# Weights in pairs of 1024 columns and a second buffer for their sums, in an attention and gated-product kernel

## Chip, core and metric

The kernel runs on one core of a Trainium2 chip. The metric is the device time of one execution in microseconds, the median of several runs. Its engines are PE (matrix products), DVE, ACT and POOL (element-wise work), and SP, whose queue issues all loads and stores.

## What is computed

Attention for 8 batches of 8 heads (576 tokens, head size 64), once over a local window and once over tokens averaged in fours, and then a gated product of the joined heads x (4608 x 512). Cut to what matters:

```python
def _attn_ref(q, k, v):
    q_d = q.reshape(B, H, Sd, factor, D).mean(axis=3)
    ...
    out_d = sm_attn(q_d, k_d, v_d)
    out_up = np.repeat(out_d, factor, axis=2)
    mask = np.abs(pos[:, None] - pos[None, :]) < factor
    scores = scale * np.matmul(q, k.transpose(0, 1, 3, 2))
    scores = np.where(mask, scores, -1000000.0)
    ...
    out_local = np.matmul(attn, v)
    return (out_up + out_local).astype(np.float32)

def _moe_ref(x, w_gate, w_val, w_out):
    gate = 1.0 / (1.0 + np.exp(-(x @ w_gate)))
    val = x @ w_val
    return (gate * val @ w_out).astype(np.float32)
```

Weights are 512 x 1536 (gate, value) and 1536 x 512 (out). They reach the kernel as 64-bit floating-point words.

## The kernel before

**Work.** A batch has four units u = 4b + hp, each a pair of heads, whose attention yields one 128-row piece of x (`xs`, split into two f16 parts). The products of a batch run over 12 pieces fc of 128 columns: `pg` (gate) and `pv` (value), 24 matmuls of 128x288 each (both halves of the tokens, 3 matmuls for each of 4 contraction pieces), then `tanh`, the product of both (L723) and its f16 split `gq` (L186 on ACT for the high part, L187 on DVE for the low one); at last the output products `po`, 72 matmuls for each of m = 0 to 3 and both halves. Batches 0 and 1 multiply plainly. Batches 2 to 7 use fewer products over block sums of the weights, which `wring` reads from a DRAM tile `wd` through a ring of three buffers.

**Weights.** There are 36 pieces (k, i), twelve each for gate, value and out. `wload` reads 512 KB (128 x 1024 32-bit words) into one of NST = 4 stage buffers. `wjoin` makes 512 f32 numbers of it: ACT's Prelu on the high word (L237), DVE's shift (L239), DVE's shift and or with the low word (L240); the largest magnitude is taken by ACT (`Abs`, L243) or by DVE (`absmax`, L182). A pair of gate and value pieces, four in all, shares a scale: `wscale` reduces the bounds to two numbers (L253), finds a power of two over all partitions through PE (`mxt`, `mxr`, `mxg`), and sets the gates' scale; `oscale` does it for the output weights. `wsplit` writes the f16 parts, high on ACT (L186), low on DVE (L187). Loads go out in the order of the joins, each new one after a join has freed a buffer.

**Sums.** In batches 0 to 2 `sums(p, k)` runs 12 times: POOL adds both parts of a pair of pieces into x (L779, 128 x 1024), DVE makes four sums of blocks in y (L788), ACT casts y to f16 back into x's place (L791), DVE subtracts for the low part (L792), and SP writes 512 KB to `wd`. There is one x and one y.

**Order.** Every step has a due time in a table T (a position, not a measured time); steps are written out sorted by it, and a scheduler with a model of the engines settles the order on each queue. `j0` to `j35` place the joins, `JBEHIND` with B1, B2, B3 and BO holds a join's shift back behind x3 or a gate product. In listings of an order `pv_1_8_0` is the value product of batch 1, fc 8, first half, and every tile has a number behind its name. Each engine works through its queue in order. The loads of q and k (`load_qk`) use NQK = 3 buffers, and a load waits for the steps `s1` and `prep2` of the unit three before.

The lines on the sum's buffers and on the order of the loads:

```python
        x = place(a, 1024)
        y = place(a + 1024, 1024)
...
    for n, prev in zip(order[NST:], order):
        add(JPOS[prev] + 0.05, lambda n=n: wload(*WORDER[n]))
```

Of the kernel before, what the change touches and what calls it, by code (L numbers as in the profile page):

```python
# [1100 lines left out]
```

## Time and profile before

| | us |
|---|---|
| median of 3 runs | 1007.38 |
| lowest, highest | 1003.67, 1007.9 |
| profiled execution | 1004.63 |
| its span | 1002.9 |
| PE busy | 972.1 (97%) |
| DVE busy | 748.3 (75%) |
| ACT busy | 576.8 (58%) |
| POOL busy | 231.6 (23%) |

The span is the time from the first to the last instruction of the profiled execution; 1.7 us of that execution lie outside it. Busy shares are means over stages of different kinds, so the stages are read one by one: the attention of batch 0 ahead of the first gate product (to 56 us), gates and values of batch 0 (to 140), its outputs (to 198), gates of batch 1 (to 281), its outputs (to 336), and six batches of 110 to 114 us. In the trace, `arena` is the room that holds the weights, x, stage and sum buffers together, `wo` the output weights, `gq` the split gated product, `x` and `od` the two attention results. A matmul record's length contains the time in which it overlaps the next one.

### The profile page before, as it was taken

The numbers are of one execution on the slowest core, as the hardware profiler recorded it, in microseconds if no ns is written. First come the engines' busy times: TensorE is split into PE (matmuls) and PEld (weight loads), VectorE is DVE, ScalarE is ACT, GpSimd is POOL, SyncE is SP. The second block draws the span as 40 slices with busy tenths as digits, with TensorE's granted clock in tenths as the row PEclk, the third lists the DMA queues.
The fourth block names the chain that finished last, engine by engine and source line by source line (L and its number), as shares of the span: only waits on it lengthen the run. The fifth ranks groups of instructions, "written<-read, shape, count | busy, mean of one in ns | idle before, by whom it ended". The sixth has DMA issues, their size and how long they took to land.

```text
span 1002.9 us, 24111 instructions
## 1 busy us (share of the span) xinstructions
PE 972.1 (97%) x9715; PEld 774.5 (77%) x9715; DVE 748.3 (75%) x1495; ACT 576.8 (58%) x1588; POOL 231.6 (23%) x244
## 2 busy tenths in 40 slices
PE   8998999999989899999999999999999999999998
PEld 6786768877767678877788778787788778887776
DVE  6998988568764899848896598948896598737750
ACT  4887677564842687437853486627963487322320
POOL 7300342414225321231203321231203210110000
PEclk9999999999989999999999999999999999999999
DMA  8668930515146355464556455463556444414501
GB/s 341 192 193 276 310 114 31 164 56 158 61 134 202 117 199 174 155 177 156 177 165 178 129 200 174 153 178 127 190 180 164 143 164 156 129 52 157 184 3 46
DMA packets 84224, 156.92 MB, mean 156 GB/s; under 512 B 43536, under 2 KB 49808, under 8 KB 84112
## 3 DMA queue, kind: packets, MB, share of 16 engines
q1 hardware_dynamic: 84112, 155.38, 48.7%
q8 instruction: 76, 1.25, 0.5%
q14 instruction: 36, 0.29, 0.1%
HBM read 127.04 MB, written 20.45 MB: 147 GB/s over the span
## 4 chain that ended last, share of the span: by engine, by line
PE 67%; DVE 12%; DMA 8%; ACT 7%; issue 3%; POOL 2%; SPq 0%; ACTq 0%; DVEq 0%; POOLq 0%
PE po L424 23%; PE pv L424 18%; PE pg L424 18%; DMA v<-in_v_dram 2%; DMA arena<-in_wg_dram 2%; PE s L460 2%; PE x L424 2%; ACT t L496 1%; PE sd L474 1%; PE od L424 1%; DVE vblk L187 1%; DVE arena L788 1%; DVE arena L832 1%; DMA wd<-arena 1%; DMA arena<-in_wv_dram 1%
## 5 line engine op out<-in xcount | busy, mean ns | idle before, releaser
L424 PEld LDWEIGHTS <-arena 128*128 128x128 f16 x4176 | 401.8, 98 | 111.8 <-issue 10.3
L424 PE MATMUL po<-gq,wo 128*128 128x288 f16 x2304 | 294.5, 289 | 5.7 <-ACT gq L186 4.6
L424 PE MATMUL pg<-arena 128*128 128x288 f16 x2088 | 274.5, 286 | 3.8 <-ACT arena L186 1.6
L424 PEld LDWEIGHTS <-wo 128*128 128x128 f16 x2304 | 225.4, 99 | 66.2 <-issue 6.0
L424 PE MATMUL pv<-arena 128*128 128x288 f16 x2088 | 275.0, 286 | 1.5 <-ACT tanh L720 0.5
L832 DVE TENSOR_TENSOR arena<-pv,arena 128x288 f32<-128x288 f32 x252 | 105.8, 450 | 23.5 <-PE pv L424 16.9
L496 ACT ACTIVATE t<-t,mx 128x64 f32<-128x64 f32 x290 | 72.5, 334 | 33.5 <-DVE mx L494 33.4
L832 DVE TENSOR_TENSOR arena<-pg,arena 128x288 f32<-128x288 f32 x180 | 76.8, 449 | 6.6 <-PE pg L424 1.7
L750 DVE TENSOR_SCALAR arena<-po,osc 128x288 f32<-128x288 f32 x32 | 16.5, 514 | 86.2 <-PE po L424 63.4
L752 ACT ACTIVATE arena<-po,osc 128x288 f32<-128x288 f32 x32 | 15.9, 500 | 86.9 <-PE po L424 80.1
L510 ACT ACTIVATE t<-t,sm 128x64 f32<-128x64 f32 x240 | 60.0, 335 | 6.8 <-DVE sm L507 5.5
L449 POOL TENSOR_TENSOR qkh<-qk 128x576 f32<-128x576 f32 x31 | 40.5, 1306 | 93.0 <-DMA qk<-in_qkd_dram 92.1
L187 DVE SCALAR_TENSOR_TENSOR vblk<-v,svb,vblk 64x640 f16<-64x640 f32 x52 | 53.2, 1023 | 6.6 <-ACT vblk L186 5.8
L407 POOL TENSOR_TENSOR vdblk<-vd 64x192 f32<-64x192 f32 x58 | 35.8, 617 | 88.0 <-PE od L424 84.9
L450 POOL TENSOR_TENSOR qks<-qkh 128x288 f32<-128x288 f32 x32 | 26.9, 840 | 113.8 <-PE sd L474 113.4
L632 ACT CAST arena<-arena 128x576 f16<-128x576 f32 (+1 forms) x24 | 21.9, 911 | 54.1 <-DVE arena L626 27.6
L186 ACT ACTIVATE vblk<-v,svb 64x640 f16<-64x640 f32 x52 | 42.8, 823 | 14.2 <-PE x L424 11.0
L535 ACT ACTIVATE e<-sd,mxd 72x144 f32<-72x144 f32 x128 | 46.8, 371 | 0.9
L405 POOL TENSOR_TENSOR vd<-vd 128x384 f32<-128x384 f32 x29 | 26.1, 901 | 88.9 <-DMA vd<-in_vd_dram 88.9
L633 DVE TENSOR_TENSOR arena<-arena 128x576 f16<-128x576 f32 (+1 forms) x24 | 28.3, 1180 | 23.4 <-ACT arena L632 23.3
L653 POOL TENSOR_TENSOR arena<-arena 128x288 f32<-128x288 f32 x12 | 9.6, 796 | 147.1 <-DVE arena L626 147.1
L779 POOL TENSOR_TENSOR arena<-arena 128x1024 f32<-128x1024 f16 x12 | 26.1, 2171 | 59.5 <-DMA wd<-arena 51.1
(140 smaller groups left out, 1331.6 us busy)
## 6 DMA issues: line engine op xcount, KB each, us to landing
arena<-wd SPq DMA_DIRECT2D x72, 896.0 KB, 4.7
qk<-in_qkd_dram SPq DMA_DIRECT2D x31, 576.0 KB, 6.2
vd<-in_vd_dram SPq DMA_DIRECT2D x29, 384.0 KB, 3.9
v<-in_v_dram SPq DMA_DIRECT2D x32, 320.0 KB, 4.5
arena<-in_wg_dram SPq DMA_DIRECT2D x12, 512.0 KB, 4.5
arena<-in_wv_dram SPq DMA_DIRECT2D x12, 512.0 KB, 5.0
arena<-in_wo_dram SPq DMA_DIRECT2D x12, 512.0 KB, 4.9
wd<-arena SPq DMA_DIRECT2D x12, 512.0 KB, 3.1
```

Source lines behind the costliest of these rows:

```text
L186: nc.scalar.activation(hi, src, AF.Copy, scale=sc)
L187: return nc.vector.scalar_tensor_tensor(out=lo, in0=src, scalar=sc, in1=hi, op0=ALU.mult, op1=ALU.subtract)
L405: nc.gpsimd.tensor_tensor(out=x[:, :, 0:2], in0=x[:, :, 0:2], in1=x[:, :, 2:4], op=ALU.add)
L407: nc.gpsimd.tensor_tensor(out=o, in0=x[ps, g, 0], in1=x[ps, g, 1], op=ALU.add)
L424: nc.tensor.matmul(o, w[a], x[c], start=first and i == 0, stop=last and i == len(pairs) - 1)
L449: nc.gpsimd.tensor_tensor(out=y, in0=x[:, :, :, 0:2], in1=x[:, :, :, 2:4], op=ALU.add)
L450: nc.gpsimd.tensor_tensor(out=s["qks"].rearrange("p (a g) -> p a g", a=2), in0=y[:, :, :, 0], in1=y[:, :, :, 1], op=ALU.add)
L496: nc.scalar.activation(t[:, g], t[:, g], AF.Exp, bias=mx[:, g : g + 1], scale=-1.0)
L510: nc.scalar.activation(t[:, g], t[:, g], AF.Copy, scale=sm[:, g : g + 1])
L535: nc.scalar.activation(s["e"][:, qb, h, :], pt[:QM, qb * SD : (qb + 1) * SD], AF.Exp, bias=mx[:, qb : qb + 1], scale=QKSCALE / 16, accum_o ...
L633: eng.tensor_tensor(out=dst_[:, :, 1], in0=src, in1=dst_[:, :, 0], op=ALU.subtract)
L832: eng.tensor_tensor(out=dst_, in0=x, in1=y, op=ALU.add)
```

## The change

- The 36 pieces become 18 pairs. `wload` reads 1 MB into two of the four stage buffers, so two loads can be under way; two are issued ahead, and each further one after a join. Join, bound and split work on 1024 columns.
- The bound of a pair is one number for gate and one for value, so the step `m2` (L253) is gone. `gate_scale` is taken out of `wscale` and placed no earlier than the maxima over v.
- The output splits run in the order 0 to 5, and the output products of batch 0 take fc in the order 0 to 11 instead of `MIXED` (0, 6, 1, 7, ...). The free gap in the output weights' room is no longer used.
- `sums` takes one of two buffers x in turn; y stays single.
- NQK falls from 3 to 2: a load of q and k waits for the unit two before. In batch 0, units 2 and 3 borrow room of the output weights.
- Unused branches of `wsplit` are deleted.
- T is set anew. Among it: T1 (start of batch 1) 193.7 to 196.29, TP 126.05 to 130.14, S0 2.49 to 3.39, SS 9.17 to 9.91, `wl` 1.41 to 9.82, B1 6 to 14, B2 14 to 3, B3 7 to 31, BO 18 to 9. With B1 = 14 no shift of a gate or value join is held back.

```diff
-NQK = 3
+NQK = 2
...
-ARENA = 2 * (NPC + 1) * WPC + 2 * NPAIR * S + NST * 2 * WPC
+ARENA = 2 * (NPC + 2) * WPC + 2 * NPAIR * S + 2 * S + 3 * 1024
...
-        turn[0] += 1
-        return place(AST + (turn[0] - 1) % NST * 2 * WPC, n)
...
+        a = turn[0] % NST
+        turn[0] += 1 if n <= 2 * WPC else 2
+        assert a + (turn[0] - a) % NST <= NST
+        return place(AST + a * 2 * WPC, n)
+
+    def wload(k, p):
+        t = wraw[k, p] = stage(4 * WPC).bitcast(I32).rearrange("p (a b) -> p a b", b=2)
+        load(t.rearrange("p (i a) b -> p i (a b)", i=2), srcs[k][2 * p : 2 * p + 2].bitcast(I32).rearrange("i p c -> p i c"))
...
-        m2 = wk.tile([P, 2 * (b - a)], F32, tag="m2", name=f"m2_{a}", bufs=2)
-        nc.vector.tensor_reduce(m2, hmx[:, 4 * a : 4 * b].rearrange("p (n f) -> p n f", f=2), axis=AX.X, op=ALU.max)
-        pow2(e, m2)
+        pow2(e, hmx[:, 2 * a : 2 * b])
         over(c, e)
-        gate_scale(0, a, b)
...
+    def wsplit(k, p):
...
+        a = wwide(k, p).rearrange("p (f c) -> p f c", f=2)
+        sc = co[:, 2 * p : 2 * p + 1] if k == "o" else cw[:, p, "gv".index(k) : "gv".index(k) + 1]
+        split(home[k][:, 2 * p : 2 * p + 2, 0], home[k][:, 2 * p : 2 * p + 2, 1], a, sc)
...
-            out_group(b, m, h, pts[h], MIXED if b == 0 else range(NFC))
+            out_group(b, m, h, pts[h], range(NFC))
...
-        x = place(a, 1024)
-        y = place(a + 1024, 1024)
+        x = place(a + (len(wready) % 2) * 1024, 1024)
+        y = place(a + 2048, 1024)
...
-        add(max(at(u - 3, "s1") + 0.1, at(u - 3, "prep2") + 0.1, p0 - T["lk"]), lambda u=u: load_qk(u))
+        add(max(at(u - NQK, "s1") + 0.1, at(u - NQK, "prep2") + 0.1, p0 - T["lk"]), lambda u=u: load_qk(u))
...
-    for n, prev in zip(order[NST:], order):
+    for n, prev in zip(order[2:], order):
         add(JPOS[prev] + 0.05, lambda n=n: wload(*WORDER[n]))
...
+        add(p0, lambda a=a, e=e: wscale(a, e))
+        add(max(p0, PV) + 0.01, lambda a=a, e=e: gate_scale(0, a, e))
...
-        add(p + 0.1 + T["os"] * i, lambda n=n: wsplit("o", n))
+    for i in range(NP):
+        add(p + 0.1 + 2 * T["os"] * i, lambda i=i: wsplit("o", i))
```

DVE's queue at the split of the last unit's x, before (`arena<-arena,cw` is a weight split, `xs<-x` the last unit's x, `arena<-xs,sxb` its split; L239 and L240 are shift and or):

```order
L187 SCALAR_TENSOR_TENSOR arena_109<-arena_109,cw_129 128x512
L161 TENSOR_SCALAR mxg4_1074<-ident_103,mxr4_1072 2x2
L187 SCALAR_TENSOR_TENSOR arena_109<-arena_109,cw_129 128x512
L626 TENSOR_TENSOR xs_113<-x_3_8_888,od16_3_880 128x112
L626 TENSOR_TENSOR xs_113<-x_3_0_887,od16_3_880 128x464
L187 SCALAR_TENSOR_TENSOR arena_109<-arena_109,cw_129 128x512 x2
L187 SCALAR_TENSOR_TENSOR arena_109<-xs_113,sxb_135,arena_109 128x576
L239 TENSOR_SCALAR arena_109<-arena_109 128x512 x4
L240 SCALAR_TENSOR_TENSOR arena_109<-arena_109 128x512 x4
```

And now (L237 and L238 are shift and or):

```order
L175 TENSOR_SCALAR cw_129<-ew_128 128x2
L287 TENSOR_SCALAR tsc_136<-ew_128,pvb_133 128x1
L608 TENSOR_TENSOR xs_113<-x_3_8_881,od16_3_878 128x112
L608 TENSOR_TENSOR xs_113<-x_3_0_880,od16_3_878 128x464
L187 SCALAR_TENSOR_TENSOR arena_109<-arena_109,cw_129 128x2x512 x2
L187 SCALAR_TENSOR_TENSOR arena_109<-xs_113,sxb_135,arena_109 128x576
L237 TENSOR_SCALAR arena_109<-arena_109 128x1024
L187 SCALAR_TENSOR_TENSOR arena_109<-arena_109,cw_129 128x2x512
L238 SCALAR_TENSOR_TENSOR arena_109<-arena_109 128x1024
```

In this stretch the four splits of 512 columns have become two of 1024 (two more stand earlier in the queue), and behind x's split four joins of 512 have become one of 1024 between two further splits.

DVE's queue at the values of fc 8 and 9 of batch 1, before (L788 and L792 are a sum's merges, `gq` the split of a gated product, L723 the product with `pv`):

```order
L626 TENSOR_TENSOR arena_109<-x_9_8_3967,od16_9_3856 128x112
L788 TENSOR_TENSOR arena_109<-arena_109 128x256 x2
L187 SCALAR_TENSOR_TENSOR gq_111<-tanh_112,gq_111 128x576
L788 TENSOR_TENSOR arena_109<-arena_109 128x256
L187 SCALAR_TENSOR_TENSOR vblk_123<-v10_2599,svb_134,vblk_123 64x10x64 x2
L788 TENSOR_TENSOR arena_109<-arena_109 128x256
L633 TENSOR_TENSOR arena_109<-arena_109 128x2x288
L723 SCALAR_TENSOR_TENSOR tanh_112<-tanh_112,pv_1_9_0_4046 128x288
L561 TENSOR_TENSOR hl_11_4215<-t_11_3722,hl_11_4215 128x640
L633 TENSOR_TENSOR arena_109<-arena_109 128x4x288
L723 SCALAR_TENSOR_TENSOR tanh_112<-tanh_112,pv_1_9_1_4059 128x288
```

And now (L769 and L773 are the sum's merges, L705 the product with `pv`):

```order
L705 SCALAR_TENSOR_TENSOR tanh_112<-tanh_112,pv_1_8_1_3821 128x288
L543 TENSOR_TENSOR hl_11_4068<-t_11_3568,hl_11_4068 128x640
L769 TENSOR_TENSOR arena_109<-arena_109 128x256 x2
L615 TENSOR_TENSOR arena_109<-arena_109 128x4x288
L182 TENSOR_REDUCE vm3_4357<-v14_4078 128x1
L769 TENSOR_TENSOR arena_109<-arena_109 128x256
L187 SCALAR_TENSOR_TENSOR gq_111<-tanh_112,gq_111 128x576
L705 SCALAR_TENSOR_TENSOR tanh_112<-tanh_112,pv_1_9_0_3897 128x288
L773 TENSOR_TENSOR arena_109<-arena_109 128x4x256
L705 SCALAR_TENSOR_TENSOR tanh_112<-tanh_112,pv_1_9_1_3910 128x288
L769 TENSOR_TENSOR arena_109<-arena_109 128x256 x3
```

One merge stands ahead of the `gq` split of fc 8 where two did, the value splits of unit 10 (`vblk`) have moved further ahead, and a sum's last step and the next sum's merges stand between and behind the products of fc 9.

DVE's queue ahead of the maximum over v of batch 2 (`mxr`, `mxg`) in the output products of batch 1, before:

```order
L788 TENSOR_TENSOR arena_109<-arena_109 128x256 x4
L505 TENSOR_REDUCE sm_12_4622<-t_12_4354 128x10
L792 TENSOR_TENSOR arena_109<-arena_109 128x4x256
L507 RECIPROCAL sm_12_4622<-sm_12_4622 128x10
L750 TENSOR_SCALAR arena_109<-po_1_2_1_4418,osc_137 128x288
L626 TENSOR_TENSOR arena_109<-x_11_0_4466,od16_11_4330 128x464
L626 TENSOR_TENSOR arena_109<-x_11_8_4492,od16_11_4330 128x112
L159 TENSOR_REDUCE mxr11_4515<-mxt11_4513 1x1
L532 TENSOR_REDUCE mxd_12_0_4533<-sd_12_0_4525 72x2
L532 TENSOR_REDUCE mxd_12_1_4617<-sd_12_1_4526 72x2
L161 TENSOR_SCALAR mxg11_4517<-ident_103,mxr11_4515 1x1
```

And now:

```order
L487 TENSOR_REDUCE sm_12_4476<-t_12_4190 128x10
L489 RECIPROCAL sm_12_4476<-sm_12_4476 128x10
L543 TENSOR_TENSOR hl_12_4513<-t_12_4190,hl_12_4513 128x640
L732 TENSOR_SCALAR arena_109<-po_1_2_1_4244,osc_137 128x288
L608 TENSOR_TENSOR arena_109<-x_11_0_4306,od16_11_4205 128x464
L608 TENSOR_TENSOR arena_109<-x_11_8_4332,od16_11_4205 128x112
L514 TENSOR_REDUCE mxd_12_0_4367<-sd_12_0_4359 72x2
L514 TENSOR_REDUCE mxd_12_1_4375<-sd_12_1_4360 72x2
L159 TENSOR_REDUCE mxr11_4385<-mxt11_4383 1x1
L615 TENSOR_TENSOR arena_109<-arena_109 128x2x288
L161 TENSOR_SCALAR mxg11_4387<-ident_103,mxr11_4385 1x1
```

The sum (L788 and L792) that stood in front is gone from here, and a step of x (L615) stands between `mxr` and `mxg`.

## Rows read from the trace of the kernel before

**Rows 1.** Windows: length, busy us of PE PEld DVE ACT POOL, PEclk, DMA share, GB/s.

```profile
56.00:140.00 84.00, 78.21 (x689) 60.38 (x687) 74.97 (x167) 63.40 (x158) 18.51 (x16) 1.00 0.75 245
140.00:198.00 58.00, 56.55 (x651) 45.54 (x650) 43.80 (x102) 35.90 (x104) 20.18 (x24) 0.97 0.30 97
198.00:281.00 83.00, 81.10 (x814) 64.63 (x812) 59.98 (x108) 57.90 (x170) 27.83 (x22) 1.00 0.34 99
281.00:336.00 55.00, 45.44 (x415) 34.51 (x414) 36.25 (x61) 21.76 (x55) 23.27 (x20) 0.91 0.49 156
336.00:450.00 114.00, 113.49 (x1156) 90.90 (x1154) 89.31 (x178) 68.53 (x197) 25.03 (x28) 1.00 0.53 171
```

**Rows 2.** Timeline of PE: start us, us, operation, count, [idle before and releaser].

```profile
55.99 2.37 PE L424 MATMUL pg<-arena 128*128 128x288 f16 x18
...
197.76 3.11 PE L424 MATMUL pg<-arena 128*128 128x288 f16 x24
200.71 2.49 PE L424 MATMUL pv<-arena 128*128 128x288 f16 x19
...
290.09 7.86 PE L424 MATMUL po<-gq,wo 128*128 128x288 f16 x39 [4.62 <-ACT gq L186]
...
329.24 0.38 PE L162 MATMUL mxt<-mxg,ones 1*128 1x1 f32 x2 [2.95 <-DVE mxg L161]
...
336.00 2.25 PE L424 MATMUL pg<-arena 128*128 128x288 f16 x17
```

**Rows 3.** Timeline of DVE around the split of x3.

```profile
56.27 1.40 DVE L187 SCALAR_TENSOR_TENSOR arena<-arena,cw 128x512 f16<-128x512 f32 x2
57.59 0.81 DVE L187 SCALAR_TENSOR_TENSOR arena<-xs,sxb,arena 128x576 f16<-128x576 f32 x1
58.32 1.43 DVE L239 TENSOR_SCALAR arena<-arena 128x512 int32<-128x512 int32 x4
```

**Rows 4.** Timeline of DVE, the merges of sums (L788, L792).

```profile
230.86 2.71 DVE L788 TENSOR_TENSOR arena<-arena 128x256 f32<-128x256 f32 x3 [0.99 <-POOL arena L779]
...
280.22 1.93 DVE L788 TENSOR_TENSOR arena<-arena 128x256 f32<-128x256 f32 x2 [4.28 <-POOL arena L779]
...
283.34 0.41 DVE L788 TENSOR_TENSOR arena<-arena 128x256 f32<-128x256 f32 x1
...
289.24 1.22 DVE L792 TENSOR_TENSOR arena<-arena 128x1024 f16<-128x1024 f32 x1
...
322.48 2.06 DVE L788 TENSOR_TENSOR arena<-arena 128x256 f32<-128x256 f32 x4 [5.74 <-POOL arena L779]
```

**Rows 5.** Timeline of POOL, two adds of sums.

```profile
278.06 2.12 POOL L779 TENSOR_TENSOR arena<-arena 128x1024 f32<-128x1024 f16 x1 [7.68 <-DMA wd<-arena]
...
293.26 2.12 POOL L779 TENSOR_TENSOR arena<-arena 128x1024 f32<-128x1024 f16 x1 [10.46 <-DMA wd<-arena]
```

**Rows 6.** Waits of POOL and of DVE, 190 to 346: us in total, times, longest.

```profile
POOL arena L779 <- DMA wd<-arena: 51.1, 9, 10.5
...
DVE arena L788 <- POOL arena L779: 18.7, 8, 5.7
```

**Rows 7.** Groups by form, DVE to 140 and ACT to 200: count, busy, mean ns, idle before.

```profile
L240 DVE SCALAR_TENSOR_TENSOR arena<-arena 128x512 int32<-128x512 int32 x24 | 17.0, 722 | 0.0
L239 DVE TENSOR_SCALAR arena<-arena 128x512 int32<-128x512 int32 x24 | 10.6, 451 | 3.5 <-ACT arena L237 3.5
...
L182 DVE TENSOR_REDUCE hmx<-arena 128x1 f32<-128x512 f32 x6 | 4.0, 675 | 0.0
...
L237 ACT ACTIVATE arena<-arena 128x512 f32<-128x512 f32 x36 | 24.3, 676 | 24.3 <-DMA arena<-in_wg_dram 9.9 <-DMA arena<-in_wo_dram 8.3 <-DMA arena<-in_wv_dram 5.9
```

**Rows 8.** DMA issues to 140: count, KB each, median us to landing.

```profile
arena<-in_wg_dram SPq DMA_DIRECT2D x12, 512.0 KB, 4.5
```

**Rows 9.** Chain of waits, 60 to 130: start us, us, what.

```profile
64.03 7.25 DMA arena<-in_wg_dram
...
88.97 3.41 DMA arena<-in_wg_dram
```

More of the change, by code (lines that the diff above doesn't have):

```diff
@@ L272, in oscale @@
         nc.vector.tensor_scalar(out=so, in0=eo, scalar1=1.0 / WUP, scalar2=ev, op0=ALU.mult, op1=ALU.mult)
-        done.update(("s", "o", i) for i in range(NPC))
+        done.update(("s", "o", p) for p in range(NP))
         out_scale(0)
-    def wsplit(k, i):
-        assert ("s", k, i) in done and ((k, i - 1) in done or i == 0 or wslot(k, i) > wslot(k, i - 1) + 1)
-        a = wwide(k, i)
-        hi, lo = (home[k][:, wslot(k, i), e] for e in range(2))
-        sc = co[:, i : i + 1] if k == "o" else cw[:, i // 2, "gv".index(k) : "gv".index(k) + 1]
-        if k == "o":
-            split(hi, lo, a, sc)
-        elif T.get(f"ws{WORDER.index((k, i))}", T["ws"]):
-            split(hi, lo, a, sc)
-        else:
-            e = T[f"mu{WORDER.index((k, i))}"]
-            if e == 1:
-                nc.scalar.activation(a, a, AF.Copy, scale=sc)
-            else:
-                (nc.gpsimd if e else nc.vector).tensor_scalar(out=a, in0=a, scalar1=sc, scalar2=None, op0=ALU.mult)
-            nc.scalar.copy(hi, a)
-            nc.gpsimd.tensor_tensor(out=lo, in0=a, in1=hi, op=ALU.subtract)
-        done.add((k, i))
+    def wsplit(k, p):
+        assert ("s", k, p) in done and (p == 0 or (k, 2 * p - 1) in done)
+        a = wwide(k, p).rearrange("p (f c) -> p f c", f=2)
+        sc = co[:, 2 * p : 2 * p + 1] if k == "o" else cw[:, p, "gv".index(k) : "gv".index(k) + 1]
+        split(home[k][:, 2 * p : 2 * p + 2, 0], home[k][:, 2 * p : 2 * p + 2, 1], a, sc)
+        done.update((k, 2 * p + i) for i in range(2))
     pvb = cp.tile([P, B], F32, tag="pvb", name="pvb")
@@ L616, in av_local @@
             s["xs"] = xs2 if b >= 2 and u % 2 else xs1
-            assert b < 2 or all(("a", k, i) in done for k in "gvo" for i in range(NPC))
+            assert b < 2 or all(("a", k, p) in done for k in "gvo" for p in range(NP))
             own(s["xs"], u)
@@ L738, in out_group @@
         for fc in fcs:
-            product(pt[:, :HN], [wo16[:, wslot("o", fc), a, m * P : (m + 1) * P] for a in range(2)],
+            product(pt[:, :HN], [wo16[:, fc, a, m * P : (m + 1) * P] for a in range(2)],
                     [gq[:, fc, e, h * HN : (h + 1) * HN] for e in range(2)], fc == FIRST[b], fc == LAST[b])
@@ L743, in out_evict @@
         osb = place(AST + 2 * S * 0 + (m % 2) * S, S) if b else stage(S)
-        assert b == 0 or all(("a", k, i) in done for k in "gvo" for i in range(NPC))
+        assert b == 0 or all(("a", k, p) in done for k in "gvo" for p in range(NP))
         if m == 3:
@@ L754, in out_evict @@
             nc.sync.dma_start(out[c, m // 2][:, m % 2, o : o + n], osb[:, i : i + n])
-    MIXED = [n // 2 + NPC // 2 * (n % 2) for n in range(NFC)]
     FIRST = {b: 0 for b in range(B)}
-    LAST = {b: MIXED[-1] if b == 0 else NFC - 1 for b in range(B)}
+    LAST = {b: NFC - 1 for b in range(B)}
     def moe_out(b, m):
@@ L774, in sums @@
         hm = whome[k]
-        assert all((k, 2 * p + i) in done for i in range(2)) and all(("a", k, i) in done for k in "gvo" for i in range(NPC))
+        assert all((k, 2 * p + i) in done for i in range(2)) and all(("a", k, p) in done for k in "gvo" for p in range(NP))
         a = AST + 2 * S
-        x = place(a, 1024)
-        y = place(a + 1024, 1024)
+        x = place(a + (len(wready) % 2) * 1024, 1024)
+        y = place(a + 2048, 1024)
         whole = nc.gpsimd.tensor_tensor(
@@ L936, in attention_moe @@
     known = {}
+    PV = min(T["vx"], min(T[f"p{i}x"] for i in range(NPAIR)) - 2) + 0.4 * (NPAIR - 1)
     for u in range(NU):
@@ L955, in attention_moe @@
     JPOS, JBEHIND = [], []
-    for n, (k, i) in enumerate(WORDER):
+    for n, (k, p) in enumerate(WORDER):
+        i = 2 * p
         JPOS.append(T[f"j{n}"])
```

64 lines of the change are left out of this document (28 added, 36 removed).

## The prediction

> **What bounds the kernel now.** I read the busy shares by stage first [rows 1]. From 336 us on TensorE (PE) is busy 113.49 of 114 us, so the batches from 2 on can only repeat their own matmul time. What can be won or lost lies ahead of 336: PE stands idle 5.8 us of the stretch 56 to 140 (gate and value products of batch 0), 1.5 us in 140 to 198 (its output products), 1.9 us in 198 to 281 (gates of batch 1) and 9.6 us in 281 to 336 (its output products). In the last one the granted clock is 0.91 besides, that is 0.09 x 55 = 5 us of clock, together 14.6 us. Then I read PE's order in time [rows 2]: products start at 55.99, 197.76 and 336.00, 24 of them take 200.71 - 197.76 = 2.95 us; at 290.09 stands a wait of 4.62 us for ACT's half of a split, behind which 39 products take 7.86 us where 39/24 x 2.95 + 0.16 = 5.0 would do, and at 329.24 a wait of 2.95 us for `mxg`, a step of the maximum over v.
>
> Both waits lead into VectorE (DVE), which takes its queue in order. [Rows 4] show it: before 280.22 DVE stood 4.28 us for POOL's whole sum of a weight pair, and before 322.48 another 5.74 us; what PE waits for is queued behind these. [Rows 5, 6] give the cause: POOL itself stood 51.1 us in nine waits for the write of the sum before it, out of the one buffer x. Thirdly the front: the split of the last unit's x (x3) ends at 57.59 + 0.81 = 58.4 [rows 3], and DVE is packed ahead of it.
>
> **Front (up to x3).** Prices first. From 256 to 1024 columns a DVE pass grows from 0.41 to 1.22 us [rows 4], 1.05 ns a column; 512 columns more cost 0.54 us. In a packed queue the second starts 0.07 us before the first's end: two splits of 512 take from 56.27 to 57.59, 0.66 each; four shifts take 1.43 in all, 0.34 from start to start [rows 3]. So with 512 columns: shift 0.34, or 0.65 (0.722 less 0.07), split 0.66, bound by DVE 0.60 (0.675 less 0.07) [rows 7]. With 1024: or 1.19, split 1.20, bound 1.14, and for the shift, whose slope no row shows, 0.60 (between 0.34 and 0.88, if it grew by the full 0.54; the shift at 0.451 against the or at 0.722 speaks for about half a slope). Per pair of pieces a join falls from 1.98 to 1.79, a split from 1.32 to 1.20: a gain of 0.2 and 0.1 us, no more. But the order puts other amounts ahead of x3's split: before 12 joins, 4 splits and 4 bounds of 512, 12 x 0.99 + 2.64 + 2.4 = 16.9 us; now 8 joins (16 of the old ones), 4 double splits and 2 bounds, 8 x 1.79 + 4.80 + 2.28 = 21.4, and two more sets of small scale steps, 0.6. That is 5.1 us more on a queue that is full, so x3's split ends near 63.5. I take **+5 us** (0, if the idle time of the first 12 us takes it up, to +9, by the loads below).
>
> **Gates of batch 0.** What was pulled ahead is missing behind x3, and ACT is relieved as well: its first step of a join takes 0.676 us and waited 24.3 us in sum for the loads [rows 7]. PE's idle time here is 5.8 us; the joins and bounds on DVE fall by 4.5 us and more behind x3, so DVE has slack against PE. I take **-4.5 us**, with ends -5.8 (all idle time) and +4 (the loads). What decides is whether weights arrive. A piece of 512 KB lands in 4.5 us in the median, with four slots [rows 8], once in 3.41 and once in 7.25 [rows 9]. Now two slots of 1 MB hold the same bytes, and a slot is refilled when the piece in it has been joined and bounded. No row shows 1 MB: between 4.5 us (latency alone) and 9.0 us (two pieces in a row). I take 5.5 to 6, nearer to the lower end, since four pieces shared the engines in the rows as well. A slot's round is then 5.6 + about 4.2 for Prelu, shift, or and bound, + 1.5 for issue and queue, some 11.3 for two slots, 5.6 us a piece. Ahead of the split of pair 3 stand seven joins behind x3's split, about two of them landed by then: 63.5 + 2 x 1.8 + 5 x 5.6 = 95. PE asks for it after 6 of 12 fc, 60 + 6 x 5.9 = 95. So it is a dead heat, and each us more of landing costs 2.5 us here. "DMA: Bandwidth & Descriptors", a page of the Trainium skill, gives in "Measured (HBM→SBUF, 128 partitions, SWDGE, issued from GpSimd)" 6.15 us for a transfer of 1 MB and advises batching to 1 MiB; no run here shows that size yet, and at 6.15 the sum would be some 1 us worse, an estimate.
>
> **Output products of batch 0.** Six double splits take the place of twelve (6 x 0.1 us less), the outputs' scale chain starts earlier in PE's order, and the fixed order of fc needs the splits in the order in which they come. Idle time and clock (0.03 x 58 = 1.7) make 3.2 us [rows 1]; I take **-2.5** (0 to -3.2).
>
> **Batch 1.** With two buffers x POOL may add the next sum while the last is still merged and written. POOL's adds of 2.12 us stand behind waits of 7.68 and 10.46 us for the write [rows 5]: from an add's start to its write's landing pass 9.8 to 12.6 us, so two buffers allow one sum in 5 to 6 us. The order now has 8 of 12 sums done by the value product of fc 4 and all 12 before batch 2 (11 before); no sum stands any more right ahead of the split of fc 9 whose POOL part is late, and none ahead of `mxr` and `mxg`. The 4.62 us, the 2.9 us of slow clock behind it, and the 2.95 us go: 10.5, of which I take **-9** since shorter waits come next in this chain (the last evictions and x of unit 11). Ends 0 and -14.6. The gates of batch 1 get three more sums, 3 x (4 x 0.41 + 1.22) = 8.6 us of DVE against 83 - 60 = 23 us of idle DVE [rows 1]: **0** in the middle, -1.9 to +4. The loads of q and k, now with two buffers, are due 19 us ahead of their unit, and units are 110/4 = 27 us apart: nothing, up to +1. From batch 2 on only steps are set anew behind a saturated PE: 0 +- 2. The later scale steps of the gates wait for nothing new.
>
> **Sum.** +5 - 4.5 - 2.5 + 0 - 9 = -11 against the profiled execution's own 1004.6 us (span 1002.9 and 1.7 around it): 993.6. That execution lies 2.8 under the median of the three runs shown; the next median should stand 1 or 2 above the sum, so I say 995.
>
> **Rivals.** *The loads are too slow for two slots* (slower, 0.16). Landing L of 1 MB enters twice: eight joins stand ahead of x3, five waiting ones ahead of pair 3. At L = 9 a piece takes (9 + 4.2 + 1.5)/2 = 7.35: x3 at about 5 + 8 x 7.35 + 3 = 67 (+8.6), gates 5 x 1.75 = 8.8 worse than forecast (+4.3), 1004.6 + 8.6 + 4.3 - 2.5 - 9 = 1006. From about L = 9.5 it is slower; at 10.5 x3 comes at 73 (+14.6), gates +8, 1016. For it: 7.25 for half the size once, and the 24.3 us that ACT waited. Against it: the median of 4.5. In between, L of 7.5 to 9 with half of the cover, ends at 1001 to 1006, within the bound (0.10).
>
> *DVE becomes the bound in the first gates of batch 1* (0.20, about half of it faster). POOL's adds now lie beside DVE's merges more often. In [rows 4] three merges (of POOL's sum, from SBUF) took 2.71 us at 230.86, while POOL worked on k and vd of a later unit,, where one alone takes 0.41: 1.5 us more for three. Over seven sums that is 10.5 us; by the order and the row means DVE needs 50 of PE's 54 us from fc 10 to fc 5, so 6.5 us come through: 1000. "GPSIMD Engine Reference" of the Trainium skill, section "1. Specifications", says the same of this pair: the SBUF interfaces are shared with VectorE, with contention where its instruction has two SBUF inputs; it speaks against this change, and the row above agrees.
>
> *All cover holds* (0.13): front +2, gates -5.8, outputs -3.2, batch 1 -13: 984.6.
>
> *The second x buffer changes nothing*, because the write to DRAM or SP's queue holds back the sums and not the buffer: POOL's wait of 51.1 would stay, and with the front at +5 and the gates at -4.5 the time is 1002; I count it in the case of 1001 to 1006.
>
> **How the numbers follow.** Forecast 995 with its own range 989 to 999: 0.41. Faster by over 0.5% (5 us, about what a measurement of this kernel can tell from no change): 0.41 + 0.13 + 0.09 = 0.63. Within: 0.11 + 0.10 = 0.21. Slower: 0.16. The range from 984 (the full gain) to 1009 (L a little over 9) leaves out about 2 in 10.
>
> **What would show it.** Front: first `pg` at 60 to 61 instead of 55.99, with DVE full up to x3. Gates: output products of batch 0 start at 140 as before, weights wait at ACT's Prelu less than 24 us, a 1 MB load lands in under 6.5 us. Batch 0 ends near 195 (197.76). Batch 1: POOL's wait for the write falls well below 51.1, DVE's 18.7 below 8, no PE wait over 2 us between 270 and 330, clock near 1.0, batch 2 starts near 325 instead of 336.00. Wrong would be: x3 later than 67, merges of 0.9 us through the whole of batch 1, or any stage from batch 2 on that is off by over 2 us.

## The result

The changed kernel takes 991.44 us in the median (990.45 to 993.02, 4 runs) against 1007.64 (1003.67 to 1009.33, 4 runs): a ratio of 0.9846 with a 95% interval of 0.9814 to 0.9878. Its profiled execution took 990.45 us, with a span of 988.4, a clock of 0.995, and the same 9715 matmuls. PE's busy time fell from 972.1 to 966.1 us.

The forecast was 995 with 984 to 1009. The time lies 3.6 us below the forecast, and behind that stand larger differences that cancel. The table gives the length of each stage in us, from the start of the first product of one to that of the next (the gates of batch 0 end with the start of their last value product, the whole with the start of the last output product).

| stage | before | changed | difference | forecast |
|---|---|---|---|---|
| front | 56.0 | 64.3 | +8.3 | +5 |
| gates, batch 0 | 84.1 | 77.3 | -6.8 | -4.5 |
| outputs, batch 0 | 57.7 | 54.1 | -3.6 | -2.5 |
| gates, batch 1 | 83.5 | 90.0 | +6.5 | 0 |
| outputs, batch 1 | 54.7 | 40.1 | -14.6 | -9 |
| batches 2 to 7 | 663.0 | 658.8 | -4.2 | 0 |
| sum | 999.0 | 984.6 | -14.4 | -11 |

### The profile page after: what moved, and what is told of

It is laid out like the page before. It is cut to its first block, busy times and chain, and to the rows that moved or that the text cites. A ratio compares the mean times of both kernels' runs of the same rounds, so it can differ in the third digit from the quotient of the medians.

```text
span 988.4 us, 23956 instructions
## 1 busy us (share of the span) xinstructions
PE 966.1 (98%) x9715; PEld 772.0 (78%) x9715; DVE 752.1 (76%) x1428; ACT 567.0 (57%) x1515; POOL 240.3 (24%) x248
## 4 chain that ended last, share of the span: by engine, by line
PE 84%; DVE 6%; DMA 3%; ACT 3%; issue 2%; POOL 1%; SPq 0%; ACTq 0%; DVEq 0%
PE po L406 29%; PE pg L406 22%; PE pv L406 22%; PE od L406 2%; PE s L442 2%; PE x L406 2%; PE sd L456 2%; DMA arena<-in_wo_dram 1%; PE adt L567 1%; PE awake L88 1%; DMA arena<-in_wg_dram 1%; DVE arena L769 1%; DVE arena L773 1%; DVE arena L238 1%; DMA v<-in_v_dram 1%
## 5 line engine op out<-in xcount | busy, mean ns | idle before, releaser
L406 PE MATMUL po<-gq,wo 128*128 128x288 f16 x2304 | 288.4, 286 | 0.0
L478 ACT ACTIVATE t<-t,mx 128x64 f32<-128x64 f32 x280 | 70.2, 335 | 53.9 <-DVE mx L476 53.9
L492 ACT ACTIVATE t<-t,sm 128x64 f32<-128x64 f32 x240 | 59.9, 337 | 13.3 <-DVE sm L489 13.3
L187 DVE SCALAR_TENSOR_TENSOR vblk<-v,svb,vblk 64x640 f16<-64x640 f32 x52 | 58.1, 1117 | 5.9 <-ACT vblk L186 4.9
L431 POOL TENSOR_TENSOR qkh<-qk 128x576 f32<-128x576 f32 x30 | 35.7, 1189 | 92.0 <-DMA qk<-in_qkd_dram 90.6
L186 ACT ACTIVATE vblk<-v,svb 64x640 f16<-64x640 f32 x52 | 42.9, 824 | 13.5 <-PE x L406 7.4
L635 POOL TENSOR_TENSOR arena<-arena 128x288 f32<-128x288 f32 x12 | 12.1, 1004 | 141.0 <-DVE arena L608 141.0
L821 ACT COPY arena<-pg 128x288 f32<-128x288 f32 x36 | 14.0, 389 | 41.3 <-PE pg L406 41.3
```

Source lines behind the costliest of these rows:

```text
L186: nc.scalar.activation(hi, src, AF.Copy, scale=sc)
L187: return nc.vector.scalar_tensor_tensor(out=lo, in0=src, scalar=sc, in1=hi, op0=ALU.mult, op1=ALU.subtract)
L406: nc.tensor.matmul(o, w[a], x[c], start=first and i == 0, stop=last and i == len(pairs) - 1)
L431: nc.gpsimd.tensor_tensor(out=y, in0=x[:, :, :, 0:2], in1=x[:, :, :, 2:4], op=ALU.add)
L478: nc.scalar.activation(t[:, g], t[:, g], AF.Exp, bias=mx[:, g : g + 1], scale=-1.0)
L492: nc.scalar.activation(t[:, g], t[:, g], AF.Copy, scale=sm[:, g : g + 1])
```

## The profile after

The windows of the changed kernel by its own stages, with the columns of [rows 1]:

```profile
64.00:142.00 78.00, 77.12 (x704) 60.33 (x699) 64.73 (x116) 58.51 (x122) 14.68 (x15) 1.00 0.74 241
142.00:196.00 54.00, 54.00 (x644) 43.99 (x642) 37.79 (x76) 35.54 (x100) 21.96 (x25) 1.00 0.32 103
196.00:286.00 90.00, 83.55 (x820) 65.60 (x819) 81.32 (x140) 54.40 (x143) 39.90 (x30) 0.98 0.40 126
286.00:326.00 40.00, 40.00 (x412) 32.22 (x410) 26.04 (x50) 20.19 (x55) 16.06 (x15) 1.00 0.42 137
326.00:440.00 114.00, 114.00 (x1166) 91.39 (x1165) 91.80 (x177) 70.10 (x201) 25.29 (x28) 1.00 0.56 171
```

PE is now full in the outputs of batch 1, 40.00 of 40 us at a clock of 1.00, where 45.44 of 55 at 0.91 stood before. The idle time of PE has moved one stage ahead: 90 - 83.55 = 6.5 us in the gates of batch 1, where DVE is busy 81.32 of 90 us (59.98 of 83 before). PE's order in time (start, length, operation, count, wait) has the borders and the waits:

```profile
64.29 2.38 PE L406 MATMUL pg<-arena 128*128 128x288 f16 x18
...
195.69 3.11 PE L406 MATMUL pg<-arena 128*128 128x288 f16 x24
...
235.77 0.32 PE L406 MATMUL x<-at,vblk 128*128 128x58 f16 x6 [2.93 <-DVE tanh L705]
...
243.21 0.71 PE L456 MATMUL sd<-qks 64*72 64x144 f32 x6 [2.72 <-DVE t L464]
...
285.65 4.57 PE L406 MATMUL po<-gq,wo 128*128 128x288 f16 x36
...
325.79 3.10 PE L406 MATMUL pg<-arena 128*128 128x288 f16 x24
```

The waits of 4.62 and 2.95 us in the outputs [rows 2] are gone. In their place stand waits of 2.93 and 2.72 us in the gates, both for DVE: one for the product with `pv` (L705), one for the masked scores `t` (L464). The waits around the sums (us in total, times, longest) answer [rows 6]:

```profile
POOL arena L760 <- DMA wd<-arena: 30.0, 6, 9.9
...
DVE arena L769 <- POOL arena L760: 3.2, 2, 2.3
```

POOL waits 30.0 instead of 51.1 us for the write, and DVE 3.2 instead of 18.7 us for POOL. What that bought, what it cost, and which of the two waits the second buffer moved, the experiments take apart.

The prices of the longer steps came out as worked out. Groups by form of the changed kernel, DVE up to 140 us:

```profile
L187 DVE SCALAR_TENSOR_TENSOR arena<-arena,cw 128x1024 f16<-128x1024 f32 x12 | 15.2, 1276 | 0.0
L238 DVE SCALAR_TENSOR_TENSOR arena<-arena 128x1024 int32<-128x1024 int32 x12 | 15.1, 1256 | 0.1
...
L237 DVE TENSOR_SCALAR arena<-arena 128x1024 int32<-128x1024 int32 x12 | 8.6, 714 | 1.9 <-ACT arena L235 1.9
```

A split of 1024 columns takes 1.28 us (forecast 1.27), the shift and or 1.26 (1.26 with its 0.07), the shift 0.71 (0.67). The loads of 1 MB, with the median from issue to landing in the last column:

```profile
arena<-in_wg_dram SPq DMA_DIRECT2D x6, 1024.0 KB, 5.4
arena<-in_wv_dram SPq DMA_DIRECT2D x6, 1024.0 KB, 5.4
arena<-in_wo_dram SPq DMA_DIRECT2D x6, 1024.0 KB, 6.1
```

5.4 to 6.1 us, where 5.5 to 6 was taken. The 6.15 us of "DMA: Bandwidth & Descriptors" of the Trainium skill (section "Measured (HBM→SBUF, 128 partitions, SWDGE, issued from GpSimd)") lies close to the loads of the output weights, though it is for a load issued from GpSimd, and these are issued from SP with another one under way.

## Experiments

Two quantities below are worked out from the traces. *DVE work* is DVE's busy time up to the end of the gates of batch 0: 121.8 us before, 114.4 changed. *Excess beside POOL* is, over the DVE instructions that run while POOL computes, the sum of what each takes beyond the length that the shortest fifth of the same operation stay under. In the gates of batch 1 it is 6.7 us before and 16.0 changed. Ratios are to the kernel before, timed anew beside each group of runs (medians 1007.1 to 1009.8 us). Stage lengths come from one profiled execution of each kernel.

### One buffer again

```diff
-        x = place(a + (len(wready) % 2) * 1024, 1024)
+        x = place(a, 1024)
```

> The changed kernel with one x buffer for the sums, all else as changed. Theory (the second buffer is what empties the output products of batch 1): POOL's wait for the write of the sum before rises from 30 us to 45 or more, the output products of batch 1 take 46 to 52 us instead of 40.2, its gates 1 to 4 us less than 89.9; the time is 4 to 9 us above the changed kernel. Rival (the new order did it, the buffer does nothing): within 2 us of the changed kernel.

Measured: 1001.17 us (997.53 to 1003.37), ratio to before 0.9941 (0.9916 to 0.9967), some 9.7 us above the changed kernel. In its profiled execution, the longest of the eight, the outputs of batch 1 take 46.7 us instead of 40.1, its gates 90.7, the batches behind it 4 us more, the gates of batch 0 2 us more. Of DVE's and PE's waits from 190 to 346:

```profile
DVE arena L769 <- POOL arena L760: 14.4, 7, 3.0
...
PE mxt L162 <- DVE mxg L161: 4.0, 1, 4.0
```

The wait for POOL is back (14.4 us), and so is PE's for `mxg` (4.0 us): in this order the second buffer takes 6.6 us out of the outputs. But two expectations failed. POOL's wait for the write stayed at 30.7 us, so nearly all of its fall from 51.1 came with the new order and not with the buffer. And the gates did not get shorter. With one buffer the excess beside POOL is only 8.0 us, yet DVE then stands waiting for POOL instead; either way the gates are about 7 us longer than before. The time lies a little above the 4 to 9 us that were expected.

### Two buffers alone

The edit is in the kernel before; its lines that find the room for the second buffer are left out here.

```diff
-        x = place(a, 1024)
-        y = place(a + 1024, 1024)
+        x = place(a + (len(wready) % 2) * 1024, 1024)
+        y = place(a + 2048, 1024)
```

> The kernel before with two x buffers alone (the room comes from a small tile of zeros that is laid into the weights' room). Theory: the output products of batch 1 lose 5 to 10 of 54.7 us, the gates of batch 1 grow by 2 to 4, the time falls by 2 to 6 us. Rival (only the new order with earlier sums can use the second buffer): within 2 us of the kernel before.

Measured: 1001.87 us (998.65 to 1005.5), ratio 0.9967 (0.9945 to 0.9988). Windows of its gates and outputs of batch 1:

```profile
198.00:290.00 92.00, 84.97 (x827) 67.11 (x825) 76.66 (x123) 60.93 (x177) 40.07 (x25) 0.96 0.32 105
290.00:331.00 41.00, 40.16 (x412) 32.12 (x411) 30.52 (x53) 19.88 (x53) 16.43 (x16) 1.00 0.61 187
```

The outputs fall from 54.7 to 41.2 us, the gates rise from 83.5 to 91.2, with an excess beside POOL of 15.7. Both moved further than expected. So the pattern of batch 1 in the changed kernel, outputs emptied and gates lengthened, comes with the second buffer in the old order too: -13.5 + 7.7 = -5.8, against -8.1 in the changed kernel.

With the run before, this makes a square. Gates and outputs of batch 1 together take 138.2 us before, 132.4 with the second buffer alone, 137.4 with the rest of the change alone and 130.1 with both: the buffer brings 5.8 to 7.3 us, the rest 0.8 to 2.3. From 190 to 346 DVE waits for POOL's sum 18.7, 2.7, 14.4 and 3.2 us in these four, which goes with the buffer; POOL waits for the write 51.1, 43.8, 30.7 and 30.0, which goes mostly with the order.

### Steps of 512 columns again

```diff
-        nc.scalar.activation(h.bitcast(F32), h.bitcast(F32), AF.Prelu, scale=WORDS, alpha=-(2.0 ** 32))
+        for c in (slice(0, 512), slice(512, 1024)):
+            nc.scalar.activation(h[:, c].bitcast(F32), h[:, c].bitcast(F32), AF.Prelu, scale=WORDS, alpha=-(2.0 ** 32))
...
-        split(home[k][:, 2 * p : 2 * p + 2, 0], home[k][:, 2 * p : 2 * p + 2, 1], a, sc)
+        for i in range(2):
+            split(home[k][:, 2 * p + i, 0], home[k][:, 2 * p + i, 1], a[:, i], sc)
```

The lines of the join on DVE, halved in the same loop, are left out. Both edits first, then the joins alone and the splits alone.

> The changed kernel with its loads and places, but ACT's and DVE's steps of join and split in two halves of 512 columns (the bound stays one). Theory (fewer, longer steps give DVE and ACT the slack that shortens the gates of batch 0): front +1 to +2, gates of batch 0 and its outputs +2 to +4, in all 3 to 6 us above the changed kernel. Rival (only the places and loads matter): within 1.5 us.

> The changed kernel with the joins' steps on ACT and DVE in halves of 512 columns, splits whole. The run with both in halves was 15 us slower with 8.1 us more DVE work up to the end of the gates of batch 0. Theory (18 joins x 0.2 us of DVE and x 0.2 us of ACT, most of it on the path since DVE is the limit there): DVE work +3 to +5, end of the gates of batch 0 +4 to +8 us, time 995 to 1000. Rival (the order that the scheduler makes of it counts, not the work): end of the gates within 2 us or over 10 us late.

> The changed kernel with the weights' splits in halves of 512 columns, joins whole. Theory: DVE work +2 to +3, ACT as much, end of the gates of batch 0 +2 to +5 us, output products +1, time 994 to 998, so that both halves add up to about the 15 us. Rival (the order counts): end of the gates within 1 us or over 8 us late.

| | time | ratio to before | front | end of gates, batch 0 | DVE work |
|---|---|---|---|---|---|
| changed | 991.44 | 0.9846 | 64.3 | 141.6 | 114.4 |
| joins in halves | 1004.42 | 0.9974 (0.9946 to 1.0002) | 66.4 | 152.3 | 119.9 |
| splits in halves | 1002.50 | 0.9949 (0.9917 to 0.9981) | 65.4 | 149.3 | 118.4 |
| both | 1006.52 | 1.0002 (0.9981 to 1.0023) | 72.3 | 155.7 | 122.5 |

With both undone the whole gain is gone in the time, though not where it was made: the front is 8.0 us longer than in the changed kernel, the gates of batch 0 6.1, its outputs 1.4, batches 2 to 7 2.1, while batch 1 keeps all that it gained. The work grew by more than 18 joins at 0.2 and 18 splits at 0.1 us (joins +5.5, splits +4.0, both +8.1 us of DVE, partly excess beside POOL; kernels here without such an edit lie between 113.8 and 116.9), and the gates end 10.7, 7.7 and 14.1 us later, close to twice the work. The two do not add up either. All three expectations were too small: by its own terms the run with the joins in halves falls to its rival (over 10 us late), the one with the splits in halves lies between theory and rival. So the longer steps matter far more in this order than the 0.2 and 0.1 us a piece at which the prediction counted them; but the runs do not separate the work from the new order that the scheduler makes out of changed durations. Other kernels here with edits that have no such work in them end these gates between 1 us sooner and 7 us later than the changed one, so order alone can make part of it.

### The front

The sum had 5 us for the front, and 8.3 came. DVE did what was worked out: up to x3's split it is busy 53.7 us instead of 49.2. But it is also idle for 14.5 instead of 9.2, so x3's split ends at 68.2, 9.8 us later than before:

```profile
67.35 0.81 DVE L187 SCALAR_TENSOR_TENSOR arena<-xs,sxb,arena 128x576 f16<-128x576 f32 x1
```

That is past the 67 that the prediction named as a sign of being wrong. The first gate product starts ahead of it, since the products of the other pieces of x come first. The chain of waits of the changed kernel, its piece from 45 us on (start, length, what):

```profile
45.41 0.60 DVE arena L237
46.24 4.39 POOL ad L534 x2
...
51.58 0.57 PE adt L567 x6
52.15 2.40 PE awake L88 x16
54.55 1.44 PE od L406 x6
...
59.40 2.18 PE awake L88 x20
```

The normalizing step of unit 2's averaged attention runs on POOL. It starts 7 us later than before, since in the chain its input stands behind splits, a bound and joins on DVE, and takes 4.39 us for two passes, where it took 2.31 before and unit 0's two take 1.29. The first pass lasts 3.76 us, while DVE runs passes with two inputs in SBUF one behind the other up to 49.5. Then empty products stand in the chain with 2.40 and 2.18 us (`awake`: they multiply a tile of zeros, only to keep PE busy). Two kernels take these away. The first changes one entry of T.

```diff
-ae2=0
+ae2=2
```

> The changed kernel with the normalizing step of unit 2's averaged attention on DVE instead of POOL, where it took 4.38 us at 46.24. Theory (this POOL step, slowed beside DVE, is the part of the front's delay that the sum missed, +8.3 where +5 was forecast): the first gate product starts at 61 to 62.5 instead of 64.3, the time is 2 to 3 us lower. Rival (the front hangs on DVE's queue of joins and on the loads): first product within 0.7 us of 64.3 or later, the time within 1 us.

Measured: 995.41 us (995.01 to 996.24), ratio 0.9894 (0.9876 to 0.9913). The first gate product starts at 61.5, as expected, but the gates of batch 0 then take 82.6 instead of 77.3 and end 2.5 us later than in the changed kernel, and the time rises by 4 us instead of falling. The chain of waits of this kernel up to 122 us:

```profile
109.90 5.41 DMA arena<-in_wo_dram
...
115.39 1.15 ACT arena L235
116.56 1.23 DVE wo L237
117.81 1.44 DVE wo L238
119.24 1.00 DVE gq L187
120.24 0.73 DVE vm L182
...
121.22 0.50 DVE t L464
...
121.77 0.71 PE sd L456 x6
```

The last piece of the output weights lands at 115.3, is joined, and behind its join on DVE stands the masked score `t` of an attention unit of batch 1, for which PE waits 2.76 us at 121.77; the granted clock from 122 to 145 is 0.93. An earlier front was worth nothing here, where the stream of weights and DVE's queue did not end earlier.

```diff
-AW = dict(s0=2, s1=2, sm=4, d0=3, a0=3, vd=8, at=12, a1=2, v=5)
+AW = dict(s0=2, s1=2, sm=4, d0=3, a0=3, vd=3, at=3, a1=2, v=2)
```

> The changed kernel with fewer of the empty products that keep PE busy in the attention of batch 0 (behind steps vd, at and v). Theory (they stand in PE's queue ahead of the transposes and products that x3 waits for): first gate product 2 to 5 us before 64.3, with a lower granted clock before it. By the run with unit 2's step on DVE this is given back, since the end of the gates of batch 0 hangs on the weights' loads and joins: their end within 1.5 us of 141.6, the time within 2 us. Rival (the gates simply follow the front): their end and the time fall by 2 to 5 us.

Measured: 999.80 us (997.37 to 1001.56), ratio 0.9927 (0.9902 to 0.9953). Here both theories failed: the front ends at 68.8, 4.5 us later. The window from 20 us to its first gate product, this kernel and then the changed one:

```profile
20.00:69.00 49.00, 34.25 (x374) 26.29 (x373) 38.11 (x81) 31.82 (x81) 19.91 (x14) 0.81 0.53 186
```

```profile
20.00:64.00 44.00, 36.87 (x427) 30.12 (x426) 38.82 (x87) 31.74 (x81) 17.78 (x14) 0.92 0.54 189
```

The granted clock is 0.81 instead of 0.92. With fewer empty products PE is busy 4.89 us of 40 to 50 (7.30 in the changed kernel), and from 50 to 69 the granted clock is 0.68. But the chain of waits of this kernel shows a second cause:

```profile
54.40 7.32 DMA arena<-in_wv_dram
...
64.27 0.42 ACT adt L541
...
64.73 1.81 PE od L406 x6
66.54 2.32 PE x L596 x40
```

In the order that came out of the edit a weight load stands on the chain, and behind its join's step on ACT the copy `adt`, for which PE waits 3.22 us. So `od` starts at 64.73 instead of 62.05, 2.7 of the 4.5 us. The last products of `od` and `x` that x3 needs, at the lower clock, then take 1.81 and 2.39 us instead of 1.00 and 1.38, the other 1.8. That the empty products lie on the changed kernel's chain does not make them a cost; what they are worth this run does not show, since the order changed with them.

### The stores beside the loads

```diff
-        with tc.issue_after(whole):
+        with tc.issue_after(wlast[0]):
             nc.sync.dma_start(wd[r][:, : 8 * P], home[k][:, 2 * p].rearrange("p e c -> p (e c)"))
```

Here `wlast` holds the load of the last piece of weights.

> The changed kernel with the copies of split weights to DRAM (24 stores, 4.5 MB, beside the weight loads from 39 to 118 us) held on SP behind the last weight load. Theory (the stream of weight loads through two slots sets the end of the gates of batch 0, and these stores take bandwidth from it): a 1 MB load lands in 4.2 to 5.2 us instead of 5.4 to 6.1, the gates of batch 0 end 1.5 to 4 us earlier, the time falls by 1 to 4 us. Rival (a slot's round is set by the join's steps on ACT and DVE): end of gates within 1 us, time within 1.5 us.

> Late copies and unit 2's normalizing step on DVE together. Theory (two limits in series: the front and the stream of loads): first gate product at 61 to 62.5, gates' end at 138 to 140, time 2 to 5 us below the changed kernel. Rival (neither is the limit, DVE's amount of work is): gates' end at 141 to 144 as in the run with that step alone, time not below the changed kernel.

Measured: 997.82 us (996.15 to 998.37), ratio 0.9894 (0.9834 to 0.9954), for the late stores; 991.23 us (989.57 to 992.93), ratio 0.9834 (0.9784 to 0.9885), with unit 2's step on DVE besides. The loads of output weights land in 5.6 and 5.1 us instead of 6.1, those of gate weights in 5.7 and 5.6 instead of 5.4. The gates of batch 0 end at 146.6 in the first and 141.9 in the second, 141.6 in the changed kernel. For the first both theory and rival failed: only the value loads landed as fast as expected (5.0 us), and the end is 5 us later. For the second the rival holds. So moving the stores neither sped up the loads much nor brought the end forward. It is no clean test, since in the second kernel's chain a load of v for batch 1 stands behind the stores on SP. The same edit costs 6.4 us in the changed kernel and gains 4.2 beside the step on DVE, so differences of this size can come from the order alone. Fronts of 64.3, 61.5 and 61.8 us led to ends of 141.6, 144.1 and 141.9: a front up to 2.8 us earlier did not end the gates sooner. What part DVE's queue and the loads' round have in this end stays open.

### Sums spread over the gates

```diff
+        hold = SPACE[len(wready)]
+        with behind(hold if hold is None else ("g", 1, (hold + 10) % 12)):
+            merges(A, Y, x, y)
...
+    SPACE = [None, 0, 1, 2, 4, 5, 6, 7, 9, 10, 11, 11]
```

> The changed kernel with DVE's merges of each sum held behind the gated product's split of a set piece of batch 1 (about one sum in 9 us), so that the sums spread over the gates and reach into the output products. Theory (the gates of batch 1 take 90 instead of 83.5 us because the sums crowd into their first 65 us, where POOL's adds slow DVE): gates of batch 1 84 to 87, output products 40 to 43, time 2 to 5 us below the changed kernel. Rival (the same work and the same slowing only move): gates fall by less than 1.5 or the output products give it back, time within 1.5 us or above.

Measured: 996.45 us (995.45 to 997.6), ratio 0.9886 (0.9836 to 0.9936). The first half of the gates of batch 1 got 6 us shorter (its middle at 238.2 instead of 243.8), the second half 10 us longer; the stage takes 93.6 us, the excess beside POOL is 19.2. The rival holds: the slowing moves with the sums.

### The adds on DVE instead of POOL

DVE in the gates of batch 1 of the changed kernel (start, length, operation, count), and POOL at the same times:

```profile
197.73 3.52 DVE L769 TENSOR_TENSOR arena<-arena 128x256 f32<-128x256 f32 x3 [0.39 <-DMA out_dram<-arena]
...
206.52 2.70 DVE L187 SCALAR_TENSOR_TENSOR vblk<-v,svb,vblk 64x640 f16<-64x640 f32 x1
...
214.71 2.75 DVE L773 TENSOR_TENSOR arena<-arena 128x1024 f16<-128x1024 f32 x1
...
221.69 1.74 DVE L773 TENSOR_TENSOR arena<-arena 128x1024 f16<-128x1024 f32 x1
...
237.47 1.22 DVE L773 TENSOR_TENSOR arena<-arena 128x1024 f16<-128x1024 f32 x1
...
251.53 2.67 DVE L769 TENSOR_TENSOR arena<-arena 128x256 f32<-128x256 f32 x2
```

```profile
198.21 2.31 POOL L760 TENSOR_TENSOR arena<-arena 128x1024 f32<-128x1024 f16 x1
206.41 2.13 POOL L760 TENSOR_TENSOR arena<-arena 128x1024 f32<-128x1024 f16 x1 [5.90 <-DMA wd<-arena]
214.24 2.14 POOL L760 TENSOR_TENSOR arena<-arena 128x1024 f32<-128x1024 f16 x1 [5.70 <-DMA wd<-arena]
...
220.21 2.14 POOL L760 TENSOR_TENSOR arena<-arena 128x1024 f32<-128x1024 f16 x1 [1.78 <-DVE tanh L705]
...
251.31 2.62 POOL L760 TENSOR_TENSOR arena<-arena 128x1024 f32<-128x1024 f16 x1 [1.04 <-DVE mxd L514]
```

The subtract of a sum (L773) takes 1.22 us at 237.47, alone, and 2.75 at 214.71, while POOL's add of 2.14 us runs from 214.24. A value split (`vblk`) takes 2.70 us at 206.52 beside the add at 206.41, alone 0.87. Three merges take 3.52 us at 197.73, where 1.1 is usual. POOL's adds stretch only little (2.1 to 2.6).

The rows show more than a slowing. The subtract at 214.71 ends at 217.46, 1.08 us behind POOL's add (214.24 + 2.14 = 216.38); the one at 221.69 ends at 223.43, again 1.08 behind the add at 220.21, though it takes 1 us less. In the whole trace of the changed kernel all five subtracts that begin during a POOL instruction end 1.08 us behind it, all 20 value splits 0.67 to 0.68, nine of ten merges 0.28 to 0.33. Such a pass looks as if it began only when POOL's ended; it costs what is left of POOL's instruction. Products with `pv` (L705, 128x288), which lies in PSUM, take their usual 0.42 to 0.46 us beside POOL. "GPSIMD Engine Reference" of the Trainium skill, section "1. Specifications", has contention on the shared SBUF interfaces for VectorE's instructions with two SBUF inputs. The subtracts, merges and value splits are such, and the trace agrees.

```diff
-        whole = nc.gpsimd.tensor_tensor(
+        whole = nc.vector.tensor_tensor(
```

> The changed kernel with the whole sum's add (12 passes of 128x1024) on DVE instead of POOL. It adds about 1.2 us of DVE work a sum and takes away the slowing of DVE beside POOL's adds (16 us of excess in the gates of batch 1 by the trace). Theory (that excess is what the gates of batch 1 lost): the excess falls to 4 to 8 us, the gates of batch 1 take 83 to 87 us instead of 90, the time falls by 2 to 6 us. Rival (the gates are short of DVE time whichever engine adds): gates 88 to 93, time within 2 us of the changed kernel or above.

> The whole sum's add on DVE together with late copies and unit 2's step on DVE. If the gates of batch 1 gain (theory of the run before), the gains add up: 985 to 989. If not, 990 to 994.

Measured: 989.30 us (986.66 to 994.21), ratio 0.9806 (0.9761 to 0.9851); together with the late stores and unit 2's step on DVE 988.86 us (988.34 to 989.74), ratio 0.9794 (0.9769 to 0.9820). The gates of batch 1 take 84.9 and 84.7 us instead of 90.0, the outputs 40.5, and the excess beside POOL falls from 16.0 to 6.3 and 6.8. DVE's groups by form from 195 to 330, with the add on DVE and then in the changed kernel:

```profile
L769 DVE TENSOR_TENSOR arena<-arena 128x256 f32<-128x256 f32 x47 | 21.3, 479 | 0.7 <-POOL arena L638 0.6
L773 DVE TENSOR_TENSOR arena<-arena 128x1024 f16<-128x1024 f32 x12 | 14.7, 1223 | 0.4 <-ACT arena L772 0.2
L760 DVE TENSOR_TENSOR arena<-arena 128x1024 f32<-128x1024 f16 x11 | 13.3, 1212 | 2.1 <-DMA wd<-arena 2.0
```

```profile
L769 DVE TENSOR_TENSOR arena<-arena 128x256 f32<-128x256 f32 x47 | 25.7, 574 | 2.2 <-POOL arena L760 0.9 <-POOL arena L638 0.6 <-DMA out_dram<-arena 0.4
L773 DVE TENSOR_TENSOR arena<-arena 128x1024 f16<-128x1024 f32 x12 | 18.8, 1563 | 4.8 <-ACT arena L772 4.6
```

The add costs DVE 1.21 us a time, 13.3 us in all. For that the mean of a subtract falls from 1.56 to 1.22 us, that of a merge from 0.57 to 0.48, and that of a value split (`vblk`) from 1.34 to 1.02. The theory holds: the gates of batch 1 lost 5 of their 6.5 us to POOL's adds beside DVE. Order alone does not explain it: in the ten kernels above with two buffers and the add on POOL this stage takes 89.8 to 93.6 us, whatever else was edited. In these two kernels the gain of the stage is partly given back in batches 2 to 6, which take some 3 us more. Both medians lie under the changed kernel's, by 2.1 and 2.6 us; by ratio the second is 0.5% under it, but both intervals still touch the changed one's, so a gain in the whole time is not shown.

## Right and wrong, step by step

**Forecast and sign** were right, by a sum whose terms were partly off: -11 forecast, -14.4 came. That the time lies so near is in part luck: the front and the gates of batch 1 came out 3.3 and 6.5 us worse than forecast, the other four terms 13.2 better.

**Front, +5 forecast, +8.3 measured.** By x3's split, which the step forecast at 63.5, it is 68.2. The amount of DVE work was right (4.5 us more, 5.1 worked out). What the step missed is that a longer queue on one engine shifts waits on others: the POOL step that took 4.39 us and PE behind it, shown by the run with that step on DVE, which starts at 61.5.

**Gates of batch 0, -4.5 forecast, -6.8 measured.** The direction is right: DVE works 60.7 us behind x3 instead of 72.6. Landing times were right (5.4 to 6.1 us), and no piece of weights stopped PE, so the rival of slow loads did not come. The size was held back for the loads; of PE's idle time 0.9 us is left, and about 1 us of its busy time went besides (77.1 in 78 us against 78.2 in 84).

**Longer steps, 0.2 and 0.1 us a piece.** The prices of single instructions were right, but undoing both costs 15 us, as much as the whole gain, so this term was mis-sized, at least in the new order. The prediction took the saving as small beside the placing, and did not ask what 8 us of DVE work are worth on an engine that was busy 121.8 of 140 us. How much of the 15 us is work and how much order stays open.

**Outputs of batch 0, -2.5 forecast, -3.6 measured.** Right in kind; PE is now busy 54.00 of 54 us.

**Gates of batch 1, 0 forecast, +6.5 measured.** The rival with DVE as the bound came true: 10.5 us of slowing over seven sums was worked out there, of which 6.5 come through, and the excess beside POOL grew by 9.3 and the stage by 6.5. That both come to 6.5 is in part luck: the rival took each merge as 0.5 us slower, where the rows look as if a pass is held until POOL's instruction ends, and its total of 1000 us did not come, since other terms were better. The row of 2.71 us [rows 4] had carried it; what failed is that it was put down as a rival with a chance of 0.2, while the sum took DVE's 23 idle us as free cover for the sums. Nor did three more sums come into the stage: it holds 35 merges instead of 27 and 8 subtracts instead of 7.

**Outputs of batch 1, -9 forecast, -14.6 measured.** That the second buffer takes out DVE's waits for POOL's sum was right and is shown by both buffer runs; that POOL's wait of 51.1 us for the write would fall with it was not, since that fell mostly with the order (30.7 us with one buffer in the new order, 43.8 with two in the old). The step kept back 1.5 of 10.5 us for shorter waits behind the ones that go, and left out the rest of the idle time and of the lost clock; nothing came in its place, and the end of the range, -14.6, is what was measured.

**Batches 2 to 7, 0 forecast, -4.2 measured.** Single waits of PE of 0.2 to 0.8 us in batches 2 to 4 are gone, 2.5 us in all, and one of 0.5 in batch 5 is new; no single batch is off by 2 us, the limit that the prediction set. In the kernels with other edits such waits are back, with nothing in those batches edited. They follow the order; no run separates what of it counts.

## What to carry to other kernels

A busy POOL is not free cover for DVE: where DVE's passes have two inputs in SBUF, price POOL's work beside them as DVE time by rows in which the two overlap, and compare it with the price of doing that work on DVE. When a change moves the work of a saturated engine between stages, give each stage its own term, and let a rival with a row behind it into the sum. A step that moves an engine's start earlier may bring nothing until the queue that ends last is shorter too. And under a scheduler that settles the order by modelled durations, undoing one part also moves others: read the chain of waits of each such run before its time is put down to the edit.
